# Row maxima of seven head pairs from the high parts alone, as 64-row products, four to a task

## Chip, core and metric

The kernel runs on one core of one Trainium2 chip. The metric is the device time of one launch in microseconds (us). The time before is 666.66 us, the median of 3 runs (666.63 to 666.75).

## The reference

Sixteen heads (two batches of eight) of pooled attention, then two dense two-layer networks over 1152 tokens of width 512:

```python
q_pool = q.reshape(B, H, S // 2, 2, D).mean(axis=3)          # 1152 queries become 576; D = 64
scores = scale * np.matmul(q_pool, k.transpose(0, 1, 3, 2))  # 576 x 1152 a head
scores = scores - np.max(scores, axis=-1, keepdims=True)
attn = np.exp(scores); attn = attn / (np.sum(attn, axis=-1, keepdims=True) + 1e-09)
out = np.matmul(attn, v)
# x = the heads side by side, 1152 x 512
# layer 1: max(0.01 h, h) with h = x @ w_in (512 x 2048), then @ w_out
# layer 2: h * sigmoid(h), same sizes
```

The maximum that is subtracted cancels in the quotient. It only has to be near enough to the row's maximum to keep the exponentials in range.

## The kernel before

The heads are worked in eight pairs p = 0 to 7; the two heads of a pair are j = 0 and j = 1. TensorE multiplies in the type fp32r, and each operand is split into a high part and a low part. For head j the tile `K2[p, j]` holds the high part of k on its own 64 rows (`own[j]`: rows 0 to 63 for j = 0, 64 to 127 for j = 1) and the low part on the other 64. `QH[p, j]` holds the high part of q twice, on both halves, so that one 128-row product gives high times high plus low times high. The own halves are written by ScalarE (ACT) from the loaded data ("at home"); the other halves come by DMA from there. `QL` and `KA` hold the low part of q, a row with minus the row maximum, and ones, for a second product.

Per pair, in the program's order of dependence:

- **Maxima** (`max_tile`, line 566). For pairs 1 to 7, 27 units, each one PSUM bank: 24 units are one product of 128 q rows by 384 keys (L586), twelve for each head; three "tail" units (L582, L583) take the last 64 q rows of both heads. VectorE (DVE) reduces each bank to one column of `mx` (L590). The q rows of a unit lie four apart (`t:NFC:NFULL`), so that the weights are read from SBUF with a stride of four elements. A unit depends on both halves of `QH` and `K2`, DMA'd parts included. `finish_max` (L634) joins three key chunks to `mn`, and a DMA writes it as a row into `QL`.
- **Scores** (`scores`, L675). Per key tile t and head two tasks of two products (128 x 288 each), then an exponential on ACT (L679) that frees the bank.
- **Sums** of the exponentials on GpSimd (POOL, L696), and at the pair's end four small products with ones (`sums`, L741).
- **Products with v** (`pv`, L712), nine tasks a pair of four fp32 products, on column halves of the array.
- `prep` loads, splits and moves q and k of a later pair; weights of the two networks are converted on ACT and DVE in the stretch of pairs 4 to 7 (L130 to L147), in part in PSUM.

The two networks follow (L1080, L1151, L1200) and are not touched.

The order of the instructions is made at build time by `Plan.run`: a list scheduler with one clock per engine, weights and due times. At each step it gives each free engine, of the tasks whose inputs and tokens are there, the one due first. PSUM banks are tokens: six "bank" tokens serve maxima, scores, sums and conversions, two further banks hold the result of `pv`. Each engine then runs its instructions in that order, waiting on semaphores.

Of the kernel before, what the change touches and what calls it, by code (L numbers as in the profile page):

```python
# [10 lines left out]
ALU = mybir.AluOpType  # L11
U32 = mybir.dt.uint32
W_TOP = 8053063168.0
AX = mybir.AxisListType
# [4 lines left out]
def pooled_attention_two_mlps(  # L19
# [27 lines left out]
    t=26.5,  # L47
# [3 lines left out]
    max=(-1.1, -0.35),  # L51
# [135 lines left out]
class Plan:  # L187
# [35 lines left out]

        self.rings[name] = (n, [], set())

    def can(self, x):
        if isinstance(x, str):
            return self.free[x] > 0
        n, taken, back = self.rings[x[0]]
        return len(taken) < n or taken[len(taken) - n] in back  # L230

    def run(self):
# [7 lines left out]
        while left:  # L240
            began = False
            for e in self.ENGINES:
                if idle[e] > now:
                    continue
                can = [t for t in ready[e] if t["at"] <= now and all(self.can(x) for x in t["take"])]
                if not can:
                    continue
                t = min(can, key=lambda t: (t["due"], t["n"]))
                for x in t["take"]:
                    if isinstance(x, str):  # L250
                        self.free[x] -= 1
                    else:
                        self.rings[x[0]][1].append(x)
                if t["emit"]:
                    t["emit"]()
                t["began"] = now
                ready[e].remove(t)
# [28 lines left out]
def attention(ctx, tc, q, k, v, xh, xl, weights, end_p):  # L286

    nc = tc.nc
# [35 lines left out]
    def bank():  # L324
        i = banks.pop(0)
        return psum[:, i], i
# [145 lines left out]
    def prep(p, loads, due, out):  # L472
# [58 lines left out]
        for j in range(2):  # L531
# [11 lines left out]
            for i in range(2):  # L543
                out["k", j, i] = a + bs
                out["kh", j, i] = a
            out["qu", j] = [cs, cs]
            out["qh", j] = cs
            out["ql", j] = [e]
        for name, ts in users.items():
# [13 lines left out]

    def max_tile(p, n, out, due):
        u, c = divmod(n, NCH)
        ks = slice(c * KC, (c + 1) * KC)
        deps = []
        for j in (0, 1) if u == NFULL else (0,) if u < NFULL else (1,):  # L570
            x = u if u <= NFULL else u - NFULL - 1

            deps += out["qu", j][0 if x < 2 else 1]
            deps += out["k", j, 0 if c == 0 else 1]

        def pe():
            if p not in mx:
                mx[p] = sm_p.tile([128, NM], F32, tag="mx", name="mx")
            box["max", p, n] = bank()
            ps = box["max", p, n][0]  # L580
            if u == NFULL:
                nc.tensor.matmul(out=ps[:, 0:KC], lhsT=QH[p, 1][:, SQ - 128:SQ], rhs=K2[p, 1][:, ks], start=True, stop=True)  # L582
                nc.tensor.matmul(out=ps[0:HALF, 0:KC], lhsT=QH[p, 0][:, NFC:SQ], rhs=K2[p, 0][:, ks], start=True, stop=True)  # L583
            else:
                j, t = (0, u) if u < NFULL else (1, u - NFULL - 1)
                nc.tensor.matmul(out=ps[:, 0:KC], lhsT=QH[p, j][:, t:NFC:NFULL], rhs=K2[p, j][:, ks], start=True, stop=True)  # L586

        def dve():
            ps, i = box.pop(("max", p, n))
            nc.vector.tensor_reduce(out=mx[p][:, n:n + 1], in_=ps[:, 0:KC], op=ALU.max, axis=AX.X)  # L590
            banks.append(i)

        t = add("PE", 0.35 if u == NFULL else 0.18, due, pe, after=deps, take=("bank",))
        return add("DVE", 0.56, due - 1.0, dve, after=[t], give=("bank",))

    def max_unit(u2, out, due, after):

# [247 lines left out]
    for p in range(NP):  # L845
# [12 lines left out]
        maxima = {}  # L858
        for u in range(2 * NFULL + 1 if p == 0 else 0):
            max_unit(u, out, 1.0 + 1.4 * u, filled[0])  # L860
        for n in range(NM if p else 0):
            lo, hi = P["max"]
            due = at(lo + (hi - lo) * n / NM)
            j, u = n // NA, n % NA // NCH
            maxima.setdefault((j, u), []).append(max_tile(p, n, out, due))
        for j in range(2 if p else 0):
            after = scored.get((p - 3, j), []) + (filled[p] if p < 3 else [])
            us = list(range(NFULL + 1 - j))
# [427 lines left out]
```

## Time and profile before

| | us |
|---|---|
| median of 3 runs | 666.66 |
| span of the profiled execution | 664.7 |
| attention, to the first product of the networks | 259.4 |
| one pair, from one set of sums to the next | 29.5 |
| PE busy | 646.1 (97%) |
| POOL busy | 392.0 (59%) |
| DVE busy | 441.3 (66%) |

The execution's own time outside its span is not shown; the median lies 2.0 us above the span. PE is TensorE, PEld its weight loads, which run under the products before. A row of the order of time gives the start, the time from the first start to the last end, the engine, the line, what is written and read, rows x columns of the weights, and how many instructions were joined. Since products overlap in the pipeline (a score product lasts 0.29 us, and the next begins 0.13 us after it), what a product costs TensorE is read from start to start, not from its length.

### The profile page before, as it was taken

How to read it: one execution, taken by the hardware profiler on the slowest of the kernel's cores; microseconds unless marked ns; L12 is line 12 of the kernel's file. 1: busy time of each engine (PE TensorE's matmuls, PEld its weight loads, DVE VectorE, ACT ScalarE, POOL GpSimd, SP SyncE). 2: the span in 40 equal slices, each digit the busy share in tenths (PEclk: the TensorE clock that was granted, in tenths of full speed). 3: DMA queues.
4: the chain of work that ended last, by engine and by line, in shares of the span. 5: the costliest groups of instructions: out<-in, count | busy, mean ns of one | idle time of the engine just before them, and what ended most of it. 6: DMA issues, size and time to landing. Idle time of an engine off the chain costs nothing.

```text
span 664.7 us, 9922 instructions
## 1 busy us (share of the span) xinstructions
PE 646.1 (97%) x3616; PEld 534.6 (80%) x3616; DVE 441.3 (66%) x614; ACT 326.8 (49%) x661; POOL 392.0 (59%) x278
## 2 busy tenths in 40 slices
PE   4889999999999998999999999999999999999997
PEld 3666777777777766988988988999988998888986
DVE  7284756678878766875676676698988888522222
ACT  4655766758686566554533433355456534312110
POOL 8657888897999833644544544476656453522120
PEclk9789999999999999999999999999999999999999
DMA  8636455455944130132233223232233322000012
GB/s 213 139 107 149 126 152 145 116 163 136 263 120 135 52 97 19 63 101 92 94 95 96 96 96 95 96 96 76 83 96 128 103 88 96 0 1 1 0 48 95
DMA packets 27959, 65.87 MB, mean 99 GB/s; under 512 B 9324, under 2 KB 9352, under 8 KB 27912
## 3 DMA queue, kind: packets, MB, share of 16 engines
q1 hardware_dynamic: 27912, 65.26, 33.7%
q8 instruction: 28, 0.46, 0.3%
q14 instruction: 19, 0.16, 0.1%
HBM read 49.81 MB, written 2.42 MB: 79 GB/s over the span
## 4 chain that ended last, share of the span: by engine, by line
PE 93%; POOL 2%; DMA 1%; ACT 1%; DVE 1%; issue 1%; SPq 0%; ACTq 0%; POOLq 0%; DVEq 0%
PE ph L1080 30%; PE po L1151 15%; PE pf L1200 15%; PE psum L675 12%; PE psum L712 11%; PE psum L586 7%; DMA k<-e 1%; PE psum L741 1%; DMA knat<-in_k_dram 1%; PE psum L583 1%; PE psum L582 1%; POOL k L439 0%; POOL e L504 0%; ACT qh L350 0%; ACT k L350 0%
## 5 line engine op out<-in xcount | busy, mean ns | idle before, releaser
L1133 POOL TENSOR_TENSOR gl<-a,gh 128x512 fp32r<-128x512 f32 (+1 forms) x64 | 97.3, 1520 | 143.1 <-ACT gh L1127 76.4
L696 POOL TENSOR_TENSOR acc<-acc,e 128x576 f32<-128x576 f32 x98 | 147.4, 1529 | 24.2 <-ACT e L679 23.8
L590 DVE TENSOR_REDUCE mx<-psum 128x1 f32<-128x384 f32 x189 | 96.5, 550 | 61.9 <-PE psum L586 55.7
L679 ACT ACTIVATE e<-psum 128x288 f32<-128x288 f32 x288 | 101.3, 414 | 69.8 <-PE psum L675 52.0
L1080 PE MATMUL ph<-xh,w0h 128*128 128x320 f32 (+1 forms) x384 | 109.0, 338 | 1.7 <-ACT pvs L727 1.7
L1080 PE MATMUL ph<-xl,w0h 128*128 128x320 f32 (+1 forms) x384 | 108.7, 337 | 0.0
L1080 PE MATMUL ph<-xh,w0l 128*128 128x320 f32 (+1 forms) x384 | 108.7, 337 | 0.0
L675 PE MATMUL psum<-qh,k 128*128 128x288 f32 x288 | 88.3, 323 | 1.7 <-ACT e L679 1.7
L712 PE MATMUL psum<-e,vnat 128*64 128x288 f32 x576 | 85.9, 423 | 0.0
L675 PE MATMUL psum<-ql,ka 128*128 128x288 f32 x288 | 81.8, 300 | 0.5 <-DMA ql<-mn 0.5
L675 PEld LDWEIGHTS psum<-qh,k 128*128 128x128 f32 x288 | 56.4, 196 | 26.3 <-issue 13.6
L1080 PEld LDWEIGHTS ph<-xh,w0h 128*128 128x128 f32 x384 | 67.7, 188 | 9.3 <-ACT pvs L727 2.2
L134 DVE TENSOR_SCALAR wt<-wt 128x512 f32<-128x512 f32 x56 | 40.3, 720 | 50.0 <-ACT wt L130 50.0
L1080 PEld LDWEIGHTS ph<-xh,w0l 128*128 128x128 f32 x384 | 66.9, 188 | 5.6
L1080 PEld LDWEIGHTS ph<-xl,w0h 128*128 128x128 f32 x384 | 66.9, 188 | 5.0
L169 POOL TENSOR_TENSOR w1l<-wt,w1h 128x512 fp32r<-128x512 f32 x32 | 44.4, 1398 | 39.1 <-ACT w1h L165 39.1
L586 PE MATMUL psum<-k,qh 128*128 128x384 f32 x168 | 62.8, 442 | 1.8 <-DMA k<-e 1.4
L169 POOL TENSOR_TENSOR w0l<-wt,w0h 128x512 fp32r<-128x512 f32 x32 | 44.7, 1396 | 24.3 <-ACT w0h L165 24.3
L138 DVE TENSOR_SCALAR wt<-wt 128x512 uint32<-128x512 uint32 x56 | 57.8, 1033 | 1.6
L712 PEld LDWEIGHTS psum<-e,vnat 128*64 128x64 f32 x576 | 35.8, 138 | 27.3 <-issue 12.0
L586 PEld LDWEIGHTS psum<-k,qh 128*128 128x128 f32 x168 | 47.1, 318 | 12.5 <-issue 4.9
L1106 ACT ACTIVATE gh<-ph 128x512 fp32r<-128x512 f32 (+1 forms) x32 | 20.9, 652 | 72.6 <-PE ph L1080 72.6
(89 smaller groups left out, 1162.8 us busy)
## 6 DMA issues: line engine op xcount, KB each, us to landing
wraw<-in_moe_w_in_dram SPq DMA_DIRECT2D x32, 512.0 KB, 3.9
wraw<-in_moe_w_out_dram SPq DMA_DIRECT2D x32, 512.0 KB, 3.3
vnat<-in_v_dram SPq DMA_DIRECT2D x8, 576.0 KB, 4.2
ka<-k SPq DMA_DIRECT2D x14, 288.0 KB, 5.2
knat<-in_k_dram SPq DMA_DIRECT2D x6, 576.0 KB, 6.0
qnat<-in_q_dram SPq DMA_DIRECT2D x6, 576.0 KB, 4.9
k<-knat SPq DMA_DIRECT2D x12, 288.0 KB, 3.3
out_dram<-acc SPq DMA_DIRECT2D x9, 256.0 KB, 2.0
```

The lines of the kernel that those rows point to most:

```text
L138: nc.vector.tensor_scalar(out=t, in0=t, scalar1=4, scalar2=1, op0=ALU.logical_shift_left, op1=ALU.logical_shift_right)
L169: self.nc.gpsimd.tensor_tensor(out=lo, in0=tf, in1=hi, op=ALU.subtract)
L586: nc.tensor.matmul(out=ps[:, 0:KC], lhsT=QH[p, j][:, t:NFC:NFULL], rhs=K2[p, j][:, ks], start=True, stop=True)
L590: nc.vector.tensor_reduce(out=mx[p][:, n:n + 1], in_=ps[:, 0:KC], op=ALU.max, axis=AX.X)
L675: nc.tensor.matmul(out=ps[:, 0:C], lhsT=lhsT[:, ks], rhs=rhs[:, cs], start=not last, stop=last)
L679: nc.scalar.activation(out=e_t[p, j, t][:, cs], in_=ps[:, 0:C], func=ACTF.Exp, scale=scale)
L696: e.tensor_tensor(out=acc[p, j], in0=e_t[p, j, 0] if t == 1 else acc[p, j], in1=e_t[p, j, t], op=ALU.add)
L712: nc.tensor.matmul(out=vps[p, c][own[j], 0:C], lhsT=vnat[p][:, j, t, :], rhs=e_t[p, j, t][:, c * C:(c + 1) * C], start=(t == 0), stop=(t = ...
L1080: nc.tensor.matmul(out=box[x][:, c, 0:n], lhsT=wt[:, kk, fs], rhs=m[:, kk, chunk(g, c)], start=(kk == 0 and wt is wh and m is xh), stop=(k ...
L1133: nc.gpsimd.tensor_tensor(out=gl, in0=box["a", x], in1=gh, op=ALU.subtract)
L1151: nc.tensor.matmul(out=box[x][:, c, 0:n], lhsT=wt[:, f, ms], rhs=y[:, c * n:(c + 1) * n], start=(f == 0 and wt is oh and y is gh), stop=(f ...
L1200: nc.tensor.matmul(out=box[x][:, 0, :], lhsT=y[:, ts], rhs=wt[:, f, :], start=(f == 0 and y is gh and wt is oh), stop=(f == FB - 1 and y i ...
```

## The change

For pairs 1 to 7 a product of the maxima (now L585) takes only the head's own 64 rows of `QH` and `K2`, which hold the high parts. Head 0 uses rows 0 to 63 of the array, head 1 rows 64 to 127. Four products, two query units of both heads for one key chunk, make one task that takes four bank tokens at once, and four tasks on DVE reduce them. So a pair has six such tasks and three tails (unchanged). The tasks depend only on the at-home halves and no longer on the DMAs. `Plan.can` is made to count tokens. The planner's weight for a task of four is 0.6, where a single product had 0.18. Numbers and sizes of products and reductions stay as they were: 168 products, 42 tails, 189 reductions.

```diff
-            out["qu", j] = [cs, cs]
+            out["qu", j] = cs
+            out["qh0", j] = [at_home["q", j]]
...
-    def max_tile(p, n, out, due):
-        u, c = divmod(n, NCH)
+    def max_tile(p, us, c, out, due):
...
+        tail = us == (NFULL,)
+        tiles = [(u, j) for u in us for j in ((1,) if tail else (0, 1))]
         deps = []
...
+        for j in range(2):
+            deps += (out["qu", j] if tail else out["qh0", j]) + out["k" if tail else "kh", j, 0 if c == 0 else 1]
...
-                nc.tensor.matmul(out=ps[:, 0:KC], lhsT=QH[p, j][:, t:NFC:NFULL], rhs=K2[p, j][:, ks], start=True, stop=True)
...
+            for u, j in tiles:
+                ps, _ = box["max", p, u, c, j] = bank()
...
+                    nc.tensor.matmul(
+                        out=ps[:, 0:KC], lhsT=QH[p, j][own[j], u:NFC:NFULL], rhs=K2[p, j][own[j], ks], start=True, stop=True,
+                    )
...
+        t = add("PE", 0.35 if tail else 0.6, due, pe, after=deps, take=("bank",) * len(tiles))
...
+        groups = [(us, c) for us in ((0, 1), (2, 3), (NFULL,)) for c in range(NCH)]
```

On TensorE, in the middle of a pair (scores of pair 3, maxima of pair 4), two places. Before (L586 maxima, L675 scores, L712 pv):

```order
L586 MATMUL psum<-k_858,qh_859 128x384 x2
L675 MATMUL psum<-qh_573,k_572 128x288
L675 MATMUL psum<-ql_104,ka_103 128x288
L675 MATMUL psum<-qh_573,k_572 128x288
L675 MATMUL psum<-ql_104,ka_103 128x288
L586 MATMUL psum<-k_858,qh_859 128x384 x2
L712 MATMUL psum<-e,vnat 64x288 x4
```

After (L585 maxima, L682 scores, L719 pv):

```order
L719 MATMUL psum<-e,vnat 64x288 x4
L585 MATMUL psum<-k_876,qh_877 128x384
L585 MATMUL psum<-k_878,qh_879 128x384
L585 MATMUL psum<-k_876,qh_877 128x384
L585 MATMUL psum<-k_878,qh_879 128x384
L682 MATMUL psum<-qh_596,k_595 128x288
L682 MATMUL psum<-ql_99,ka_98 128x288
L682 MATMUL psum<-qh_596,k_595 128x288
L682 MATMUL psum<-ql_99,ka_98 128x288
L719 MATMUL psum<-e,vnat 64x288 x4
```

Twos of one head between scores have become fours that alternate between the heads. Of the 42 tasks 30 stand right behind a pv, three behind the sums, eight behind scores or tails and one behind another task.

On TensorE where the scores of pair 5 end and those of pair 6 begin. Before, with two of pair 7's products on either side; the last product for pair 6's maxima stands 12 score tasks and three pv tasks ahead of pair 6's first score:

```order
L586 MATMUL psum<-k_1785,qh_1786 128x384 x2
L712 MATMUL psum<-e,vnat 64x288 x4
L675 MATMUL psum<-qh_1455,k_1454 128x288
L675 MATMUL psum<-ql_101,ka_97 128x288
L675 MATMUL psum<-qh_1455,k_1454 128x288
L675 MATMUL psum<-ql_101,ka_97 128x288
L586 MATMUL psum<-k_1785,qh_1786 128x384 x2
```

After (k_1457 and k_1459 are pair 6, k_1817 and k_1819 pair 7; L748 are the sums of pair 5):

```order
L719 MATMUL psum<-e,vnat 64x288 x4
L582 MATMUL psum<-k_1819,qh_1820 128x384
L583 MATMUL psum<-k_1817,qh_1818 64x384
L582 MATMUL psum<-k_1819,qh_1820 128x384
L583 MATMUL psum<-k_1817,qh_1818 64x384
L582 MATMUL psum<-k_1819,qh_1820 128x384
L583 MATMUL psum<-k_1817,qh_1818 64x384
L585 MATMUL psum<-k_1457,qh_1458 128x384
L585 MATMUL psum<-k_1459,qh_1460 128x384
L585 MATMUL psum<-k_1457,qh_1458 128x384
L585 MATMUL psum<-k_1459,qh_1460 128x384
L748 MATMUL psum<-acc,ones 32x288 x4
```

The last task of pair 6's maxima now stands behind all scores of pair 5 and behind pair 7's tails; after the sums come eight products for pair 7, and then pair 6's first score, which needs those maxima.

On DVE at the same boundary. Before, with pair 6's two joins (L634) apart:

```order
L590 TENSOR_REDUCE mx<-psum 128x1 x2
L634 TENSOR_REDUCE mn_1887<-mx 128x5
L590 TENSOR_REDUCE mx<-psum 128x1 x3
L776 RECIPROCAL cmp<-cmp 128x9
L590 TENSOR_REDUCE mx<-psum 128x1 x2
L504 TENSOR_TENSOR knat<-knat,kf 128x1152
L590 TENSOR_REDUCE mx<-psum 128x1 x4
L134 TENSOR_SCALAR psum<-psum 128x512
L634 TENSOR_REDUCE mn_1983<-mx 128x4
```

After (L594 reductions, L641 joins):

```order
L594 TENSOR_REDUCE mx<-psum 128x1 x4
L827 TENSOR_TENSOR xl<-pvs,xh 128x576
L147 SCALAR_TENSOR_TENSOR wt<-wraw,psum 128x512
L594 TENSOR_REDUCE mx<-psum 128x1 x3
L134 TENSOR_SCALAR psum<-psum 128x512
L594 TENSOR_REDUCE mx<-psum 128x1 x4
L641 TENSOR_REDUCE mn_2078<-mx 128x5
L641 TENSOR_REDUCE mn_2080<-mx 128x4
```

The reductions come in fours, and both joins stand behind the last of them.

## Rows read from the trace of the kernel before

**Rows 1.** The page: busy time and share of the span of each engine.

```profile
PE 646.1 (97%) x3616; PEld 534.6 (80%) x3616; DVE 441.3 (66%) x614; ACT 326.8 (49%) x661; POOL 392.0 (59%) x278
```

**Rows 2.** Busy time by stretch: length, five engines, granted clock, DMA share, GB/s.

```profile
63.88:93.38 29.50, 29.50 (x183) 21.42 (x182) 19.77 (x34) 19.73 (x47) 26.60 (x18) 1.00 0.47 133
181.90:211.40 29.50, 29.50 (x184) 21.60 (x183) 23.25 (x41) 21.57 (x51) 28.66 (x21) 1.00 0.49 136
```

**Rows 3.** TensorE in order of time inside one pair: start, length, line, joined.

```profile
100.94 0.67 PE L586 MATMUL psum<-k,qh 128*128 128x384 f32 x2
101.45 0.30 PE L675 MATMUL psum<-qh,k 128*128 128x288 f32 x1
...
101.84 0.29 PE L675 MATMUL psum<-ql,ka 128*128 128x288 f32 x1
102.07 1.19 PE L712 MATMUL psum<-e,vnat 128*64 128x288 f32 x8
103.19 0.80 PE L586 MATMUL psum<-k,qh 128*128 128x384 f32 x2
103.83 0.29 PE L675 MATMUL psum<-qh,k 128*128 128x288 f32 x1
...
105.23 1.19 PE L712 MATMUL psum<-e,vnat 128*64 128x288 f32 x8
106.35 0.40 PE L675 MATMUL psum<-qh,k 128*128 128x288 f32 x1
106.58 0.30 PE L675 MATMUL psum<-ql,ka 128*128 128x288 f32 x1
```

**Rows 4.** Groups by shape, weight loads: strided (L586) and contiguous (L582); mean in ns.

```profile
L586 PEld LDWEIGHTS psum<-k,qh 128*128 128x128 f32 x168 | 47.1, 318 | 12.5 <-issue 4.9 <-DVE mx L590 3.1 <-ACT e L679 2.0
L582 PEld LDWEIGHTS psum<-k,qh 128*128 128x128 f32 x21 | 3.9, 188 | 0.3
```

**Rows 5.** TensorE in order of time around two tails.

```profile
67.65 0.29 PE L675 MATMUL psum<-ql,ka 128*128 128x288 f32 x1
67.78 0.34 PE L582 MATMUL psum<-k,qh 128*128 128x384 f32 x1
67.96 0.34 PE L583 MATMUL psum<-k,qh 128*64 128x384 f32 x1
68.13 0.33 PE L582 MATMUL psum<-k,qh 128*128 128x384 f32 x1
```

**Rows 6.** The four sums of a pair in order of time, products.

```profile
63.88 0.69 PE L741 MATMUL psum<-acc,ones 128*32 128x288 f32 x8
64.50 0.57 PE L586 MATMUL psum<-k,qh 128*128 128x384 f32 x1
```

**Rows 7.** Their weight loads in order of time.

```profile
63.87 0.16 PEld L741 LDWEIGHTS psum<-acc,ones 128*32 128x32 f32 x8 [0.18 <-issue]
```

**Rows 8.** The page's costliest groups on POOL, DVE and ACT in attention.

```profile
L696 POOL TENSOR_TENSOR acc<-acc,e 128x576 f32<-128x576 f32 x98 | 147.4, 1529 | 24.2 <-ACT e L679 23.8
L590 DVE TENSOR_REDUCE mx<-psum 128x1 f32<-128x384 f32 x189 | 96.5, 550 | 61.9 <-PE psum L586 55.7
L679 ACT ACTIVATE e<-psum 128x288 f32<-128x288 f32 x288 | 101.3, 414 | 69.8 <-PE psum L675 52.0
```

**Rows 9.** TensorE in order of time at pair 1's maxima.

```profile
34.79 1.74 PE L586 MATMUL psum<-k,qh 128*128 128x384 f32 x6 [1.41 <-DMA k<-e]
```

**Rows 10.** Busy time by stretch just behind them; the clock is third from last.

```profile
36.00:40.00 4.00, 4.00 (x16) 2.48 (x16) 3.02 (x8) 1.79 (x3) 2.77 (x2) 0.57 0.26 96
```

**Rows 11.** The tile of joined maxima: its reductions, and its DMAs' issue to landing.

```profile
L634 DVE TENSOR_REDUCE mn<-mx x14: 152/156/167, 51.8 to 228.8; 128x5 fp32r<-128x15 f32 x7, 128x4 fp32r<-128x12 f32 x7
...
DMA to landing us min/median/max: 1.8/2.1/3.5
```

**Rows 12.** Groups by shape on DVE, 22 to 245 us: two of its other steps.

```profile
L820 DVE TENSOR_TENSOR xl<-pvs,xh 128x576 fp32r<-128x576 f32 x6 | 7.0, 1160 | 0.9 <-ACT xh L819 0.6
L147 DVE SCALAR_TENSOR_TENSOR wt<-wraw,psum 128x512 uint32<-128x512 uint32 x8 | 5.5, 683 | 0.2
```

More of the change, by code (lines that the diff above doesn't have):

```diff
@@ L224, in ring, with can @@
         self.rings[name] = (n, [], set())
-    def can(self, x):
+    def can(self, x, n=1):
         if isinstance(x, str):
-            return self.free[x] > 0
+            return self.free[x] >= n
         n, taken, back = self.rings[x[0]]
@@ L244, in run @@
                     continue
-                can = [t for t in ready[e] if t["at"] <= now and all(self.can(x) for x in t["take"])]
+                can = [t for t in ready[e] if t["at"] <= now and all(self.can(x, t["take"].count(x)) for x in t["take"])]
                 if not can:
@@ L561, in copy_ka @@
             out["ka", j, 0] = out["ka", j, 1] = [dma(due, go, after=out["kh", j, 0] + after, lag=P["lag"] + 1.0)]
-    def max_tile(p, n, out, due):
-        u, c = divmod(n, NCH)
+    def max_tile(p, us, c, out, due):
         ks = slice(c * KC, (c + 1) * KC)
+        tail = us == (NFULL,)
+        tiles = [(u, j) for u in us for j in ((1,) if tail else (0, 1))]
         deps = []
[L570 to L574, printed above, removed]
+        for j in range(2):
+            deps += (out["qu", j] if tail else out["qh0", j]) + out["k" if tail else "kh", j, 0 if c == 0 else 1]
         def pe():
@@ L578, in pe, with dve, go @@
                 mx[p] = sm_p.tile([128, NM], F32, tag="mx", name="mx")
[L579 to L585, printed above, removed]
-                nc.tensor.matmul(out=ps[:, 0:KC], lhsT=QH[p, j][:, t:NFC:NFULL], rhs=K2[p, j][:, ks], start=True, stop=True)
[L588 to L594, printed above, removed]
+            for u, j in tiles:
+                ps, _ = box["max", p, u, c, j] = bank()
+                if tail:
+                    nc.tensor.matmul(out=ps[:, 0:KC], lhsT=QH[p, 1][:, SQ - 128:SQ], rhs=K2[p, 1][:, ks], start=True, stop=True)
+                    nc.tensor.matmul(out=ps[0:HALF, 0:KC], lhsT=QH[p, 0][:, NFC:SQ], rhs=K2[p, 0][:, ks], start=True, stop=True)
+                else:
+                    nc.tensor.matmul(
+                        out=ps[:, 0:KC], lhsT=QH[p, j][own[j], u:NFC:NFULL], rhs=K2[p, j][own[j], ks], start=True, stop=True,
+                    )
+        def dve(u, j):
+            n = NCH * u + c + (NA if j and not tail else 0)
+            def go():
+                ps, i = box.pop(("max", p, u, c, j))
+                nc.vector.tensor_reduce(out=mx[p][:, n:n + 1], in_=ps[:, 0:KC], op=ALU.max, axis=AX.X)
+                banks.append(i)
+            return go
+        t = add("PE", 0.35 if tail else 0.6, due, pe, after=deps, take=("bank",) * len(tiles))
+        return [
+            (0 if tail else j, u, add("DVE", 0.56, due - 1.0, dve(u, j), after=[t], give=("bank",))) for u, j in tiles
+        ]
     def max_unit(u2, out, due, after):
@@ L860, in attention @@
             max_unit(u, out, 1.0 + 1.4 * u, filled[0])
-        for n in range(NM if p else 0):
+        groups = [(us, c) for us in ((0, 1), (2, 3), (NFULL,)) for c in range(NCH)]
+        for n, (us, c) in enumerate(groups if p else ()):
             lo, hi = P["max"]
-            due = at(lo + (hi - lo) * n / NM)
-            j, u = n // NA, n % NA // NCH
-            maxima.setdefault((j, u), []).append(max_tile(p, n, out, due))
+            for j, u, t in max_tile(p, us, c, out, at(lo + (hi - lo) * n / len(groups))):
+                maxima.setdefault((j, u), []).append(t)
         for j in range(2 if p else 0):
```

## Prediction

> **What bounds the kernel now.** I read the busy times first, then their shares by stretch, then TensorE's row in order of time. TensorE is busy 97% of the span [rows 1]. A middle pair takes 29.5 us, and TensorE is busy for all of it at the full clock, as it is in a late pair [rows 2]. So what a maxima product costs TensorE in a pair is what it costs the kernel, until another engine ends last. The nearest is POOL: 26.6 of 29.5 us in the middle pair, 28.7 in the late one, where it also splits weights [rows 2]. DVE and ACT stand at 19.8 and 19.7 us in the middle, 23.3 and 21.6 late.
>
> The reader is to look at starts. Two maxima products between scores begin at 100.94 and the next score at 101.45: 0.51 us for two, 0.255 each [rows 3]. A score product of 288 columns takes 0.13 us, so 384 columns alone would take 0.13 x 384/288 = 0.17 to 0.18, and the tails, also 384 columns, do take 0.17 to 0.18 [rows 5]. The difference is the weight load: with its stride of four it takes 318 ns, the contiguous one of the tails 188 [rows 4]. Maxima products go at the pace of their loads.
>
> **The change part by part.** The sum is made on the median: the profiled execution's own time is known only as its span of 664.7, 2.0 below the median, and all that changes lies inside the span.
>
> Removed: 168 products, in 84 twos. A two between scores is 0.51. Behind a pv it takes 0.64 (103.19 to 103.83), but of that the first product after a pv pays 0.10 in any case (0.23 from 106.35 to 106.58 where 0.13 is usual), so 0.54 net [rows 3]. About one two in four is of that kind: 84 x 0.5175 = 43.5 us.
>
> Added: 42 tasks of four products. Nothing in the trace has products on row halves. What one costs depends on two things.
>
> First, whether the halves run at once. The bounds are two product times or four for a task. The nearest rows are of column parts. Four products on four 32-column parts go from 63.88 to the next product at 64.50 in 0.62 us, and four of the same 288 columns on two 64-column parts from 102.07 to 103.19 in 1.12 us [rows 3, 6]. Twice as many parts take about half the time, so parts of the array do run together; the eight weight loads of the four also fit in 0.16 us [rows 7]. I take it that row halves do likewise, loads included, because a half's load then fills rows of its own as a column part's fills columns of its own. A task then costs what a two costs now: 0.51, or 0.54 behind a pv or the sums. By the order 33 tasks stand there and 9 elsewhere: 33 x 0.54 + 9 x 0.51 = 22.4 us. The gain is 43.5 - 22.4 = 21.1. If the loads of half the rows went faster than a full one, a pair of products would be bound by its 0.175 us of columns where I count 0.255; 42 x 2 x 0.08 = 7 more would be gained, and POOL's 28.7 us would not let the late pairs have all of it.
>
> Second, whether TensorE must empty itself where the shape of its parts changes. The nearest rows are the tails: there a full-width product is followed by one on 64 columns of the array and the next full one, at 67.78, 67.96 and 68.13, with steps of 0.18 and 0.17 [rows 5]. That is the pace of the columns, so the change of shape costs nothing there. Farther is the step into pv (0.23 from 101.84 to 102.07 where 0.13 is usual) and out of it (the 0.10 above) [rows 3]; those change the data type as well. I take nothing, by the nearer row; the other end is in the first rival.
>
> Moved, pair 1's start. Its maxima waited 1.41 us for the DMA k<-e, and the clock then stood at 0.57 from 36 to 40 us [rows 9, 10]. The new tasks need only the at-home copies and go among pair 0's scores; the tails that still need the DMA come after four of the tasks. That takes the wait away. Up to 1.7 of the slow stretch (4 us x 0.43) may go too, and some tasks now fall into the slow stretch before 30 us. I take -1.5 in all, between 0 and -3.
>
> Moved, the boundary of pairs 5 and 6. By the order the last task for pair 6's maxima stands behind all scores of pair 5. From the start of the task before it DVE has: 0.4 until the first product is out, four reductions (2.2), L827 (1.16), L147 (0.68), three reductions for tails (1.65), L134 (0.68 like L147), four reductions (2.2), two joins (0.3), and then the DMA lands 2.1 later [rows 8, 11, 12]. The sum is 11.4 us until pair 6's first score may start. TensorE has in that time: the task (0.54), a pv with its way in and out (1.3), three tails (3 x 0.35), the last task (0.54), the sums (0.85 with ways in and out), two tasks for pair 7 (1.1): 5.4 us. It waits 6.0. Bounds: 3 if the conversions have run early, 7.7 with a slow clock after the wait as in [rows 10].
>
> The boundary of pairs 6 and 7 has the same form with more behind it: four score tasks and two pv, 4.2 us with the task, against 0.4 + 2.2 + 0.3 + 2.1 = 5.0: 0.8. The other boundaries have three or four pv and eight to sixteen score tasks between the last maxima and the next pair's scores, over 8 us, and cost nothing.
>
> Moved, the banks. A task holds four of six banks until DVE has reduced them, 4 x 0.55 = 2.2 us [rows 8]. Scores behind it share two banks; a bank is bound for 0.27 of products, 0.41 of the exponential [rows 8] and 0.2 of handing over (an estimate, from a product that lasts 0.30 at a pace of 0.13 [rows 3]), so a score task comes every 0.44 instead of 0.27. If TensorE had only scores to do, it would lose 40% of that time. Scores fill a third of a pair (72 x 0.133 = 9.6 of 29.5), and 42 x 2.2 x 0.33 x 0.4 = 12 us is the upper end; zero is the lower, since most tasks stand behind a pv, which gives DVE and ACT 1.1 us, and about half are followed by at most two scores and then a pv or tail. I take 3.5, half a microsecond a pair.
>
> Nothing is added on DVE, ACT or the DMA queues: the same 189 reductions and the same moves. Accuracy of the maximum does not enter the time.
>
> Sum: 666.66 - 21.1 - 1.5 + 6.0 + 0.8 + 3.5 = 654.4; I say 654.5. Its own range is 645 (no bank waits, short boundary) to 662 (12 of bank waits).
>
> **The rivals.** *The array empties itself at each change of shape.* Then coming out of a task costs 0.10 of emptying, as the step into pv, and 0.10 for a first load that nothing hides, as the step out of it; this falls on all 42. The nine that don't stand behind a change of type pay 0.10 for going in, too, and 0.13 for their own strided load (0.64 against 0.51): 33 x 0.20 + 9 x 0.43 = 10.5 [rows 3]. The time is 665.0. For it: row parts are not column parts. Against it: the tails. The Trainium skill, page TensorEngine Tiling (Array Packing), section Tiling Modes, Key Properties, says that changing the tiling mode drains TensorE. By that the time would be this rival's; the tails' rows do not agree with it.
>
> *The halves do not overlap*, because loads or products of the two heads follow one another: this is the slower one. A task costs 1.05 behind a pv (0.64 + 0.51 - 0.10) and 1.02 elsewhere, 33 x 1.05 + 9 x 1.02 = 43.8, and nothing is gained: 654.5 + 21.4 = 675.9, less about 2 of bank waits that a slower TensorE hides, 674. It decides from 0.80 us a task on: the gain of 21.1 + 1.5 less the 10.3 of waits is 12.3, which is 0.29 a task over 0.53. For it: the strided load is what bounds now, and if it is bound by one reading path, halving the rows does not help. Against it: the sums.
>
> *Each task waits for a bank.* A task needs its four banks within half a microsecond, DVE gives one back every 0.55, and its other steps (1.16 and more) come in between. One reduction late per task is 42 x 0.55 = 23 instead of 3.5: 674. For it: DVE's share in late pairs. Against it: the order puts tasks behind a pv. The same page of the Trainium skill warns, under Gotcha 1, of more PSUM pressure with row tiling; no row here shows row tiles.
>
> **How the numbers follow.** My forecast has 0.52, the emptying array 0.22, no overlap 0.16, the banks 0.10. A measurement of this kernel can tell 0.2% (1.3 us) from no change. Nearly all of the first case is faster; of the second 0.12 is faster, 0.07 the same, 0.03 slower, since it lies 1.7 below with several us of doubt; the last two are slower but for 0.03. That gives faster 0.65, same 0.09, slower 0.26. Eight in ten: from 645, the low end of the forecast, to 673, which leaves out about half of the two slow cases and the deepest gains.
>
> **What would show it.** In the trace of the changed kernel the two products of heads 0 and 1 begin within some 20 ns of each other, and a task takes 0.5 to 0.55 from its first start to the next score; a middle pair takes 26.5 to 27.5 us. If a task takes 0.7 to 0.95 with the pairs of starts together, it is the first rival; if four starts lie 0.25 apart, the second; if TensorE's idle time is ended by the reductions again and again, the third. At the start of pair 6's scores there is a wait of 3 to 8 us ended by the DMA of the maxima, and none before pairs 2 to 5. The wait for k<-e is gone. I am wrong if the halves follow one another, or if waits at more boundaries than one eat the gain.

## The result, and the profile after

The changed kernel takes 669.86 us (median; 669.31 to 672.13) where the kernel before takes 666.7: ratio 1.0053, 95% interval 1.0035 to 1.007. The forecast was 654.5 us. The profiled execution has a span of 667.2 (before 664.7) and a mean clock of 0.988. Lines of the kernel after, in attention: L585 maxima, L594 their reductions on DVE, L682 scores, L686 exponentials, L719 pv, L748 sums, L703 POOL's sums of exponentials.

The page's busy line, to be set against [rows 1]:

```profile
PE 643.8 (97%) x3616; PEld 518.7 (78%) x3616; DVE 434.9 (65%) x614; ACT 324.3 (49%) x661; POOL 393.7 (59%) x278
```

TensorE is still busy 97%, and only 2 us less in all: the tasks save more, but slow stretches of the clock, shown below, make other products longer. Two tasks in TensorE's order of time (start, length, line), as [rows 3]:

```profile
93.05 1.19 PE L719 MATMUL psum<-e,vnat 128*64 128x288 f32 x7
94.16 0.80 PE L585 MATMUL psum<-k,qh 64*128 64x384 f32 x4
94.89 0.40 PE L682 MATMUL psum<-qh,k 128*128 128x288 f32 x1
95.12 0.29 PE L682 MATMUL psum<-ql,ka 128*128 128x288 f32 x1
95.26 0.29 PE L682 MATMUL psum<-qh,k 128*128 128x288 f32 x1
```

Four products take 0.73 us (94.16 to 94.89), and the first step behind them is 0.23 where 0.13 or 0.14 is usual. Inside a task the products start at 0, 0.00, 0.40 and 0.41 (medians): the two heads run at once, the second pair begins 0.40 behind the first. A task costs 0.73 behind a pv (the step of 0.23 is paid there in any case) and 0.93 between scores, where the way in takes 0.225 for 0.133 and the first score behind it pays 0.1 as well.

Then where the time goes. Until pair 5's scores begin, the changed kernel is ahead: the first scores of pairs 2 to 5 start at 84.7, 113.0, 142.6 and 172.4 us, before at 89.0, 118.5, 148.0 and 177.7, with the same 52, 76, 100 and 124 products of maxima done. Pair 6's first score is 3.9 late (211.1 for 207.2). One pair, from its first score to the next pair's, loses 9.3 us; before, then after:

```profile
177.74:207.22 29.48, 29.48 (x184) 21.48 (x183) 22.71 (x43) 21.77 (x50) 28.64 (x21) 1.00 0.59 159
```

```profile
172.40:211.14 38.74, 36.31 (x203) 23.01 (x201) 32.11 (x55) 23.07 (x54) 32.36 (x22) 0.92 0.61 164
```

Some of the 9.3 is work that stands earlier in the new order: pair 7's three tails, one more task and the sums of pair 5, about 2.4 us. The rest is waits and slow clock. TensorE in order of time at three waits, the first of them at pair 1's start, the others in that pair:

```profile
40.70 0.29 PE L682 MATMUL psum<-ql,ka 128*128 128x288 f32 x1
44.21 0.61 PE L682 MATMUL psum<-qh,k 128*128 128x288 f32 x1 [3.21 <-ACT e L686]
...
187.62 0.29 PE L682 MATMUL psum<-ql,ka 128*128 128x288 f32 x1
190.02 0.40 PE L682 MATMUL psum<-qh,k 128*128 128x288 f32 x1 [2.10 <-DVE mx L594]
...
204.20 0.56 PE L585 MATMUL psum<-k,qh 64*128 64x384 f32 x1
205.06 1.49 PE L585 MATMUL psum<-k,qh 64*128 64x384 f32 x3 [0.29 <-DVE wt L147]
206.55 1.09 PE L748 MATMUL psum<-acc,ones 128*32 128x288 f32 x8
207.56 3.65 PE L585 MATMUL psum<-k,qh 64*128 64x384 f32 x8
211.14 0.61 PE L682 MATMUL psum<-qh,k 128*128 128x288 f32 x1
```

ScalarE (ACT) ahead of the first:

```profile
38.33 0.69 ACT L350 ACTIVATE qnat<-qnat 128x576 fp32r<-128x576 f32 x1 [2.32 <-POOL qnat L480]
38.92 1.37 ACT L350 ACTIVATE qh<-qnat 64x576 fp32r<-64x576 f32 x2
40.32 1.17 ACT L350 ACTIVATE kf<-knat 128x1152 fp32r<-128x1152 f32 x1
41.39 2.33 ACT L350 ACTIVATE k<-knat 64x1152 fp32r<-64x1152 f32 x2
43.75 2.53 ACT L686 ACTIVATE e<-psum 128x288 f32<-128x288 f32 x8
```

VectorE (DVE) ahead of the second:

```profile
186.74 2.75 DVE L499 TENSOR_TENSOR qnat<-qnat 128x576 fp32r<-128x576 f32 x1
189.42 0.55 DVE L594 TENSOR_REDUCE mx<-psum 128x1 f32<-128x384 f32 x1
```

At 44.21 the score waits for a bank that an exponential frees, and the exponential stands on ACT behind pair 2's preparation, 5.4 us in a row from 38.33. Before, the same preparation began at 38.18, and TensorE had pair 1's maxima to do there [rows 9, 10]. At 190.02 the bank is freed by a reduction that stands on DVE behind a subtraction of 2.75 us. From 204.20 to 211.14 three tasks wait bank by bank for DVE, and the next pair's first score comes late. Busy time by stretch has the clock third from last, below 1.00 behind each of the three; in the other two rows nothing stops, and POOL, the fifth figure, is full:

```profile
40.00:50.00 10.00, 6.52 (x32) 3.64 (x30) 3.02 (x3) 6.92 (x14) 6.44 (x5) 0.83 0.50 118
...
70.00:80.00 10.00, 10.00 (x69) 6.91 (x65) 5.97 (x12) 7.60 (x17) 10.00 (x7) 1.00 0.66 177
...
170.00:180.00 10.00, 9.96 (x68) 5.99 (x65) 7.80 (x14) 6.91 (x18) 10.00 (x8) 1.00 1.00 224
...
190.00:200.00 10.00, 9.98 (x56) 6.32 (x56) 5.81 (x8) 5.17 (x15) 8.44 (x6) 0.83 0.65 171
...
210.00:220.00 10.00, 9.96 (x50) 7.26 (x50) 7.58 (x16) 4.72 (x12) 2.84 (x3) 0.76 0.23 55
```

### The profile page after: what moved, and what is told of

It is laid out like the page before. It is cut to its first block, busy times and chain, and to the rows that moved or that the text cites. A ratio compares the mean times of both kernels' runs of the same rounds, so it can differ in the third digit from the quotient of the medians.

```text
span 667.2 us, 9923 instructions
## 1 busy us (share of the span) xinstructions
PE 643.8 (97%) x3616; PEld 518.7 (78%) x3616; DVE 434.9 (65%) x614; ACT 324.3 (49%) x661; POOL 393.7 (59%) x278
## 4 chain that ended last, share of the span: by engine, by line
PE 90%; DVE 4%; ACT 2%; issue 1%; DMA 1%; SPq 0%; POOL 0%; ACTq 0%; DVEq 0%; POOLq 0%
PE ph L1087 30%; PE po L1158 15%; PE pf L1207 15%; PE psum L682 13%; PE psum L719 10%; PE psum L585 4%; DVE mx L594 2%; PE psum L617 1%; DVE mn L622 1%; DMA qnat<-in_q_dram 1%; PE psum L748 1%; ACT k L350 1%; ACT e L686 1%; PE psum L582 0%; DMA qh<-qh 0%
## 5 line engine op out<-in xcount | busy, mean ns | idle before, releaser
L703 POOL TENSOR_TENSOR acc<-acc,e 128x576 f32<-128x576 f32 x98 | 149.0, 1550 | 14.5 <-ACT e L686 13.9
L594 DVE TENSOR_REDUCE mx<-psum 128x1 f32<-128x384 f32 x189 | 93.1, 549 | 59.5 <-PE psum L585 49.3
L686 ACT ACTIVATE e<-psum 128x288 f32<-128x288 f32 x288 | 97.9, 420 | 64.7 <-PE psum L682 56.6
L682 PE MATMUL psum<-qh,k 128*128 128x288 f32 x288 | 91.8, 337 | 7.4 <-ACT e L686 4.7
L719 PE MATMUL psum<-e,vnat 128*64 128x288 f32 x576 | 86.8, 426 | 0.0
L682 PEld LDWEIGHTS psum<-qh,k 128*128 128x128 f32 x288 | 56.0, 195 | 34.8 <-issue 12.0
L682 PE MATMUL psum<-ql,ka 128*128 128x288 f32 x288 | 82.3, 303 | 0.0
L719 PEld LDWEIGHTS psum<-e,vnat 128*64 128x64 f32 x576 | 36.3, 138 | 28.1 <-issue 13.0
L682 PEld LDWEIGHTS psum<-ql,ka 128*128 128x128 f32 x288 | 56.6, 196 | 0.0
L1207 PE MATMUL pf<-w1h,gl 128*128 128x512 f32 x144 | 56.2, 390 | 0.0
```

The costliest lines, as they stand in the source:

```text
L682: nc.tensor.matmul(out=ps[:, 0:C], lhsT=lhsT[:, ks], rhs=rhs[:, cs], start=not last, stop=last)
L686: nc.scalar.activation(out=e_t[p, j, t][:, cs], in_=ps[:, 0:C], func=ACTF.Exp, scale=scale)
L703: e.tensor_tensor(out=acc[p, j], in0=e_t[p, j, 0] if t == 1 else acc[p, j], in1=e_t[p, j, t], op=ALU.add)
L719: nc.tensor.matmul(out=vps[p, c][own[j], 0:C], lhsT=vnat[p][:, j, t, :], rhs=e_t[p, j, t][:, c * C:(c + 1) * C], start=(t == 0), stop=(t = ...
L1207: nc.tensor.matmul(out=box[x][:, 0, :], lhsT=y[:, ts], rhs=wt[:, f, :], start=(f == 0 and y is gh and wt is oh), stop=(f == FB - 1 and y i ...
```

## Experiments

### Do the halves overlap, and what does a task cost?

All four products on rows 0 to 63:

```diff
-  lhsT=QH[p, j][own[j], u:NFC:NFULL], rhs=K2[p, j][own[j], ks]
+  lhsT=QH[p, 0][own[0], u:NFC:NFULL], rhs=K2[p, 0][own[0], ks]
```

> The changed kernel with all four products of a task on rows 0 to 63 (head 0's operands for both heads; so head 1 is shifted by head 0's maxima, which cancels in the quotient). The order of the instructions is that of the changed kernel. If products run together because they lie on different halves, the starts are 0.23 to 0.41 apart here, a task takes 1.05 to 1.3 instead of 0.73, and the kernel is 8 to 20 us slower than the changed one: 678 to 690. If two 64-row products run together wherever they lie, as the run with head by head could also mean, starts and time are those of the changed kernel, 670.

679.11 us, ratio 1.0191 [1.0173, 1.021], 9.2 slower than the changed kernel. TensorE's row:

```profile
92.33 1.26 PE L585 MATMUL psum<-k,qh 64*128 64x384 f32 x4
93.52 0.69 PE L748 MATMUL psum<-acc,ones 128*32 128x288 f32 x8
```

A task takes 1.19, its products start at 0, 0.40, 0.64 and 0.87. So the overlap comes from the two halves, as expected. Of 42 x 0.46 = 19 us of added work 9.2 reach the time.

The two products of a head one behind the other in the program:

```diff
-  tiles = [(u, j) for u in us for j in ((1,) if tail else (0, 1))]
+  tiles = [(u, j) for j in ((1,) if tail else (0, 1)) for u in us]
```

> The changed kernel with the four products of a task in the order head 0, head 0, head 1, head 1. If the halves overlap because neighbouring products lie on different halves, the first pair no longer starts together: a task takes 0.40 + 0.40 + 0.32 = 1.1 instead of 0.72, 42 x 0.4 = 16 us of TensorE's time, and the kernel is 6 to 16 us slower than the changed one. If the starts lie together for another reason, the time is the same, 669.9.

670.57, 1.0064 [1.0041, 1.0088]: no different from the changed kernel, and starts at 0, 0.01, 0.41, 0.41. The expectation's main case, 6 to 16 us slower, was a miss: the halves pair up whatever their order in the task. (The trace does not name the half of a product; that two on one half start 0.4 apart is the run before.)

### The order: tasks of four, and what they wait for

Tasks of four that wait for the moved rows, as the twos did before: in one kernel with products of all 128 rows (both edits), in another with row halves (the first edit alone):

```diff
-  deps += (out["qu", j] if tail else out["qh0", j]) + out["k" if tail else "kh", j, 0 if c == 0 else 1]
+  deps += out["qu", j] + out["k", j, 0 if c == 0 else 1]
...
-  lhsT=QH[p, j][own[j], u:NFC:NFULL], rhs=K2[p, j][own[j], ks]
+  lhsT=QH[p, j][:, u:NFC:NFULL], rhs=K2[p, j][:, ks]
```

> The changed kernel with its tasks of four and its planner, but each product of the maxima over all 128 rows as before, and the old dependence on the DMA'd halves (so the order of the instructions is that of e5_old_deps). If the order and the hold on four banks alone cost time (theory of the waits), this is slower than before by 8 to 14 us, since its products are those of before: 675 to 681. If they cost nothing, it is as before, 667. A task should take 0.25 to 0.28 a product (1.0 to 1.05 in all), its first start 0.13 behind a score, and the score behind it should pay nothing extra.

> The changed kernel with the old dependence alone: 64-row products, tasks of four, but they wait for the DMA'd halves again. Against e1_fours_full_rows only the rows differ. If halves overlap and emptying the array takes back half of it, a task takes 0.72 here against 1.0 to 1.05 there: 42 x 0.3 = 12.6 us of TensorE's time, of which the waits keep a part: 4 to 12 us faster than e1. Against the changed kernel: 0 to 4 us slower if the early start of pair 1 helps, and as much faster if it only moves the wait.

685.18, 1.0274 [1.0259, 1.029], and 680.61, 1.0214 [1.0175, 1.0252]. Grouping alone, with the products of before and the order that the planner makes of it, costs 18 us; 8 to 14 were expected. The first kernel is also the control for the change of shape. Its tasks go in and out at the usual pace (from the score behind a task to the next start it is 0.14 here, 0.24 behind row halves), and its last product takes 0.235 to the next start, where that of row halves takes 0.32:

```profile
117.97 1.27 PE L585 MATMUL psum<-k,qh 128*128 128x384 f32 x4
119.08 0.30 PE L682 MATMUL psum<-qh,k 128*128 128x288 f32 x1
119.22 0.29 PE L682 MATMUL psum<-ql,ka 128*128 128x288 f32 x1
```

Row halves save TensorE some 10 us against it (a task behind a pv takes 0.73 for 1.11, less the 0.1 of the score behind), and 4.6 reach the time. The changed kernel is 10.7 faster still, where 0 to 4 were expected; its only edit against the second is the dependence on the at-home copies, but that gives a new order throughout, so the 10.7 are not shown to be pair 1's start alone.

Tasks of two products, one of each head, that take two banks:

```diff
-  groups = [(us, c) for us in ((0, 1), (2, 3), (NFULL,)) for c in range(NCH)]
+  groups = [(us, c) for us in ((0,), (1,), (2,), (3,), (NFULL,)) for c in range(NCH)]
```

> The changed kernel with tasks of two products (one unit of both heads) instead of four: 84 tasks, two banks each. If emptying the array is the larger loss, twice as many changes of shape cost TensorE 84 x (0.32 to 0.52) = 27 to 43 us against 32 for the fours, and the time is 667 to 676. If the hold on four banks is the larger loss, the waits of some 14 us fall to 5 or less and the time is 660 to 667.

667.84, 1.0014 [1.0005, 1.0024]. Its TensorE work is about that of before or more (a two costs 0.50 and both ways, some 0.69 between scores); that fewer banks held at once make up for it is the likely reason, not shown by itself.

A planner that keeps banks free for a due task of four, so that no scores slip in ahead of it:

```diff
+  short = [x["due"] for x in ready["PE"] if x["at"] <= now and x["take"].count("bank") > 1]
+  if short and min(short) < t["due"] and t["take"].count("bank") == 1:
+      can = [x for x in can if "bank" not in x["take"] or x["take"].count("bank") > 1]
...
```

> The changed kernel with one more rule in the planner: while a task of four is ready on TensorE and due earlier, nothing due later takes a single bank. By the order at least 14 score tasks then stand between a pair's last maxima and its first scores at every boundary (0, 4 and 8 at the boundaries of pairs 6, 7 and 1 in the changed kernel). TensorE's own work stays as in the changed kernel, some 11.4 us under that of before by starts in the two traces. If starved tasks at the boundaries make the loss, the waits fall from some 14 us to 3 to 7, and the time is 658 to 662. If each task's hold on four banks makes it, wherever it stands, the time stays at 666 to 670.

672.38, 1.0088 [1.0066, 1.0111]. 658 to 662 was expected if late tasks at the pairs' boundaries make the loss. That theory fell: now 17 tasks stand between scores, they take 0.94 in the median, and nine of them wait for banks inside.

### Is POOL the next bound?

The kernel before with contiguous maxima products (a two takes 0.35 for 0.51 of [rows 3], some 13 us less for TensorE; no row halves). The edit has a second part, not shown here: the row of maxima is then written by six more DMAs a pair.

```diff
-  lhsT=QH[p, j][:, t:NFC:NFULL]
+  lhsT=QH[p, j][:, t * 128:(t + 1) * 128]
```

> The kernel before with one change: the q rows of a maxima unit are 128 neighbours, so the weight load reads without a stride; the row of maxima is then written by one DMA per unit (nine more than before reduced to four: six more DMAs a pair). If the strided load sets the pace of the 128-row products, a two between scores takes 0.35 to 0.38 instead of 0.51, 168 x 0.07 to 0.08 = 12 to 13 us go from TensorE, and the time is 653 to 658. If the load is hidden, 667. If the further DMAs come late, there are waits before each pair's scores and up to 2 us a pair come back.

665.69, 0.9991 [0.9976, 1.0005]. 653 to 658 was expected; nearly nothing of 13 us comes out, without any change of shape or grouping. That made POOL the suspect: in this kernel it is at 10.00 of 10 in eight of the 24 stretches of 10 us from 20 to 260 (in the kernel before it is in two, in the changed one in six). So 14 sums of exponentials went from POOL to DVE, in the kernel before, the changed one and the contiguous one, and 28 in the changed one:

```diff
-    dve_add=(),
+    dve_add=((1, 0), (1, 1)),
```

> The kernel before with one edit: in pairs 0 to 6 the first sum of exponentials of each head (14 in all) is made by DVE (0.75 us each) instead of POOL (1.42 each). POOL has 20 us less to do, DVE 10.5 us more, TensorE's work is unchanged. Theory that POOL becomes the bound only where TensorE is relieved: TensorE is busy 97% of this kernel, so 664 to 668, within 0.4% of 666.9. Rival (the banks: DVE gives them back later and that is what stalls the scores): 668 to 674, since DVE has more to do. If this kernel alone is faster by over 4 us, POOL bounded the kernel before already.

> The changed kernel (669.9) with the same edit: 14 sums moved from POOL to DVE. Theory that POOL is the bound once TensorE is relieved: POOL is no longer at 10.00 of 10 in window after window, the stalls of the scores behind held tiles go, and of the 11.4 us that TensorE was relieved of most comes out: 656 to 662. Rival (four banks held by a task until DVE has reduced them): DVE has 10.5 us more, banks come back later, 670 to 676.

> The kernel before with contiguous maxima products (they take 0.35 a two where they took 0.51; that alone gave 665.7) and the same edit: 14 sums moved from POOL to DVE. No tasks of four, no row halves. Theory that POOL is the bound once TensorE is relieved: 653 to 659. Rival (the order, or DVE, is the bound): 664 to 670.

> The changed kernel with twice the dose: the first two sums of each head of pairs 0 to 6 (28 in all) made by DVE; POOL has some 41 us less to do than in the changed kernel, DVE 21 more. Theory that POOL is the bound once TensorE is relieved: with two moved sums a pair POOL is already well below the span, so the other two give little: within 3 us of the kernel with 14 moved sums, 655 to 662. Rival (banks and DVE): slower again than that one by 3 to 8 us, 673 to 682.

669.07 (1.0036 [1.0021, 1.005]), 664.91 (0.9974 [0.9963, 0.9985]), 665.74 (0.9985 [0.9967, 1.0002]) and 671.53 (1.0078 [1.0058, 1.0099]). The changed kernel gains 5 us, and 8 to 14 were expected if POOL is the bound; twice the dose loses 1.7 instead; the contiguous one gains nothing, where 7 to 13 were expected. POOL is not all of it, and how much of the 5 us is POOL and how much the new order is open.

### Pair 1's start

Pair 2's loads are planned to land later, so that its preparation stands behind pair 0's last exponentials on ACT; in the changed kernel without and with the 14 moved sums, in the one with tasks of two and in the contiguous one:

```diff
+  lag = 11.0 if p == 2 else 5.0
-  made["q"] = [dma(due + 0.1, q_part(None), take=("qnat",), lag=5.0, begin=begin)]
+  made["q"] = [dma(due + 0.1, q_part(None), take=("qnat",), lag=lag, begin=begin)]
```

> The changed kernel with one edit: the planner is told that pair 2's q and k land 11 us after their issue, where it takes 5, so that pair 2's preparation on ScalarE (5.4 us in a row from 38.3) is planned behind the exponentials of pair 0's last scores and not ahead of them. Theory that the change took away cover (pair 1's maxima used to keep TensorE at work there): the wait of 3.4 at 44.2 us goes and so does about 1 us of slow clock behind it: 664.5 to 667 where the changed kernel has 669.9. Rival (another engine bounds the pairs, so that time won at one place is given back at the next): 668.5 to 671.

> Both edits in the changed kernel: pair 2's preparation planned later, and 14 sums of exponentials moved from POOL to DVE (that alone gave 664.9, with a wait of 4.3 us at 42.4). If the two causes are separate they add: 659 to 662. Rival (the moved sums had already taken what there was, another engine bounds the rest): 663.5 to 666.

> The kernel with row halves but tasks of two products and two banks (667.8, with one wait of 3.1 us at 38.9 ended by an exponential), with pair 2's preparation planned later. Theory of the lost cover: 663 to 665.5. Rival (given back later): 667 to 669.

> The kernel before with contiguous maxima products (665.7; no row halves, pair 1's maxima still behind the moved rows) and pair 2's preparation planned later. There TensorE had pair 1's maxima as cover, its waits near that place were 1.5 (a DMA) and 1.2 (an exponential). Theory of the lost cover: at most the 1.2 goes, 664 to 666.5. Rival (the plan's wrong landing time costs every kernel): 661 to 663.5.

668.55 (1.0031 [1.0019, 1.0044]), 677.45 (1.0155 [1.0131, 1.0179]), 668.97 (1.0039 [1.0014, 1.0063]) and 664.70 (0.9966 [0.9951, 0.9981]). The wait did not go, it moved. TensorE's row of the first:

```profile
45.10 0.29 PE L683 MATMUL psum<-ql,ka 128*128 128x288 f32 x1
49.68 0.61 PE L683 MATMUL psum<-qh,k 128*128 128x288 f32 x1 [4.29 <-ACT e L687]
```

In both places of ACT's 5.4 us TensorE has only scores to do, since pair 1's maxima lie earlier. And with both edits, two gains became a loss of 12.5 against the moved sums alone, where 659 to 666 was expected: each new plan shifts waits of several us.

### What would tasks at no cost give?

Products left out, all else in its order: in the kernel before every second one (the edit shown), or all of them (with p < 0 for the condition), and in the changed kernel all of pairs 2 to 7 (with p < 2).

```diff
-            else:
+            elif n % 2 == 0:
                 j, t = (0, u) if u < NFULL else (1, u - NFULL - 1)
                 nc.tensor.matmul(out=ps[:, 0:KC], lhsT=QH[p, j][:, t:NFC:NFULL], rhs=K2[p, j][:, ks], start=True, stop=True)
```

> The kernel before with every second maxima product of pairs 1 to 7 left out (84 of 168; the reductions still run, on what the bank holds, so the maxima are not the reference's; the last 96 columns of each bank are set to zero once at the start). TensorE has 84 x 0.255 = 21.4 us less to do, just the gain that the forecast put on the change; the order of every engine is the same. If TensorE is the bound: 645 to 648. If the other engines and the written order take over: 656 to 665, with TensorE waiting.

> The kernel before with all 168 maxima products of pairs 1 to 7 left out (the reductions still run on what the banks hold). TensorE has 43.5 us less to do. If TensorE is the bound: 623 to 628. If other engines and the order hold the time from some point on: 648 to 662, little below the kernel with half of the products left out.

> The changed kernel with the maxima products of pairs 2 to 7 left out (36 of 42 tasks of four; the reductions still run on what the banks hold). TensorE has 36 x 0.73 to 0.93, some 27 to 30 us, less to do and no change of shape but the tails'; the order is the changed kernel's. If TensorE is the bound: 640 to 645. If the other engines and the order hold the time: 654 to 667, in other words the changed kernel could not have been much faster even with tasks that cost nothing.

656.13 (0.9839 [0.9825, 0.9854]), 652.45 (0.9781 [0.9765, 0.9798]) and 667.20 (1.0029 [0.9997, 1.006]). One stretch, 60 to 220 us, of before, the half, all, the changed kernel, and that with its products left out (TensorE, its loads, DVE, ACT, POOL, clock):

```profile
60.00:220.00 160.00, 160.00 (x988) 116.44 (x987) 118.00 (x204) 110.05 (x257) 138.61 (x94) 1.00 0.55 148
```

```profile
60.00:220.00 160.00, 157.99 (x982) 107.53 (x982) 124.20 (x221) 113.82 (x270) 150.96 (x101) 1.00 0.57 152
```

```profile
60.00:220.00 160.00, 149.84 (x939) 93.50 (x939) 125.11 (x222) 115.09 (x279) 154.19 (x105) 0.98 0.57 151
```

```profile
60.00:220.00 160.00, 155.81 (x963) 102.16 (x962) 112.79 (x205) 106.33 (x251) 137.64 (x92) 0.97 0.57 151
```

```profile
60.00:220.00 160.00, 135.44 (x842) 85.62 (x842) 119.42 (x207) 106.22 (x254) 136.16 (x92) 0.95 0.58 157
```

In the order of before, 21.4 us less work (by the forecast's price of 0.255; a product left alone between scores takes 0.28, so nearer 20) gives 10.7, the next 22 give 3.7, and POOL goes from 87% to 94% and 96%. With all left out POOL is what bounds the pairs. TensorE's longest sum of waits in these 160 us is at the pairs' sums, for POOL (what waits, what ends it, us in total, times, longest):

```profile
PE psum L741 <- POOL acc L696: 6.3, 7, 1.6
```

With half left out it is not: TensorE is busy for 158 of the 160 us, and none of its waits there is ended by POOL. Some 4 us of what is missing are lost at pair 1's start, where there are fewer maxima to cover ACT's preparation (before, then the half; the clock is third from last):

```profile
40.00:50.00 10.00, 9.62 (x44) 7.18 (x44) 9.96 (x19) 6.68 (x12) 5.13 (x3) 1.00 0.28 58
```

```profile
40.00:50.00 10.00, 7.84 (x28) 5.25 (x28) 7.34 (x15) 5.86 (x10) 3.53 (x3) 0.68 0.32 70
```

Pair 1's first score starts at 60.2 us for 59.5 before, though 14 products fewer stand ahead of it. What keeps the other 5 or so is not shown.

In the changed order, 27 to 30 us less work gives 2.7, and no engine is above 85%. There the order itself holds the time, with waits for DVE, ACT and POOL in turn, and the clock with it: it stands at 0.95 over the stretch, where the changed kernel has 0.97 and the kernel before 1.00, so up to 8 of the 160 us go with slow stretches. The waits in the whole of this run:

```profile
PE psum L682 <- DVE mx L594: 9.6, 6, 6.2
PE psum L682 <- ACT e L686: 9.4, 10, 2.7
...
PE psum L748 <- POOL acc L703: 5.1, 6, 2.5
```

## Why the forecast was wrong

**The halves run at once**: right. Starts are 3 ns apart, and with one half alone the task takes 1.19 for 0.73. By the forecast's own signs (pairs of starts together, a task of 0.7 to 0.95) it is the first rival that came.

**The array does not empty**: wrong. I priced the change of shape at nothing by the tails, which use fewer columns [rows 5]; products on row halves pay 0.09 from the last pair to the next start, 0.1 at the score behind, and between scores 0.09 on the way in and 0.40 for 0.255 at the first pair; full rows in the same tasks pay none of the ways in and out. (The 0.40 is not of the halves: a full-width product behind the sums takes it too, 64.50 to 64.90 before [rows 6].) 33 x 0.73 + 9 x 0.93 = 32.5 us for 22.4: the gain for TensorE is 11.0 and not 21.1. That is the first rival, 10.5 priced, 10.1 measured, and its parts fit too (0.19 a task for 0.20, 0.42 for 0.43 for the nine). The Trainium skill, page TensorEngine Tiling (Array Packing), section Tiling Modes, Key Properties, says that a change of the tiling mode drains TensorE. The tasks agree with it by 0.1 each way, the tails still do not.

**"What a maxima product costs TensorE in a pair is what it costs the kernel, until another engine ends last"**: this would have failed even with tasks as cheap as forecast, for I priced every us of TensorE's work as a us of time. Half of the products left out, about the gain of 21 that I forecast, gives 10.7, and all of them 14.4: a gain of 21 was not there to be had by cheaper products alone. I named POOL for the engine that ends last and gave it no price; it is that engine only with all left out. [Rows 2] did not have the cap: POOL leaves 2.9 us in that middle pair and 0.8 in that late one, but over 60 to 220 us it leaves 160 - 138.6 = 21.4, more than came out. With half left out, some 4 us were lost at pair 1's start, and the rest is open. In the changed kernel the middle pairs, forecast at 26.5 to 27.5, take 28.3, 29.6 and 29.8 from first score to first score, where 29.5 stood before.

**Pair 1's start**, -1.5: right in sign, about a third of the size, and by other waits than forecast. The wait of 1.41 went [rows 9], but the maxima that went with it were what TensorE did during ACT's preparation: there 3.2 us of waits came, and 0.3 ahead of them. What paid for it was not in the forecast: in the kernel before the first scores wait 0.55 for a DMA and 1.65 for an exponential (at 21.5 and 23.6 us), and pair 1's first task now runs in that place. TensorE's waits from 20 to 60 us, but for one of 0.4 that both have, are 4.0 before and 3.5 after; slow stretches are alike in both (at about 24 to 29 us before and 21 to 27 after, by the pace of the scores, and again behind 36.5 and 44.2), so about -0.5.

**The boundary of pairs 5 and 6**, +6.0: about right (204.2 to 211.1 for work of some 3 us, and the stretch at 0.76 behind it). **Banks held**, +3.5: the rows of TensorE show some 2.7 us at 102, 127 to 132 and 150. **A wait behind DVE's preparation**, at 190: 2.1 us and about 1.2 of slow clock, not forecast.

With these sizes the forecast's own sum is 654.4 + 10.1 + 1.0 (pair 1's start) + 3.3 (at 190) = 668.8, and 669.9 was measured. The nearness is in part luck, for the terms do not simply add: with the tasks at no cost the changed kernel keeps 667.2. Its order is 14.8 slower than that of before when both have their products left out (652.45; the changed kernel still has pair 1's six tasks, 4.4 to 5.6 us, and a clock of 0.95 for 0.98 over 60 to 220 us). So the emptying is what the rival said, and yet in the changed order even tasks at no cost would give little, for waits that the order makes stand behind it. Up to pair 5 the changed kernel was 5.3 us ahead; the waits at 190 and from 204 to 211 lost that and more. What share each cause has (four banks held until DVE has reduced them, a pair's last task behind the scores before, preparation ahead of reductions) stays open: each attempt to take one away moved the waits.

Two versions beat both kernels: the changed one with 14 sums on DVE (664.91), and, without row halves, the contiguous products with pair 2's preparation later (664.70).

## What to carry to other kernels

Before pricing relief of the busiest engine, leave the work out and measure: here leaving out half gave half of its price, and the other half 3.7 us. The room of the second busiest engine, summed over the stretches, is an upper bound only (21.4 us here, 14.4 came out). Before moving work earlier, look what long step of another engine it covers where it stands. Compare two orders where equal work is done: a loss that looks spread may sit in one pair. And price a change of the array's parts by rows of the same kind of part: the tails, a change of columns at no cost, did not tell the cost of a change of rows.

## What the runs showed of the hardware

A VectorE sum or difference of 128 x 576 with both inputs in SBUF takes 0.75 us while POOL is idle (all 18 at the end of attention in the changed kernel). While POOL works it takes 0.75 to 1.9 in the kernel before, the changed one and that with its products left out, and in two cases far longer: 2.75 and 6.87. In the changed kernel with its products left out, DVE in order of time:

```profile
181.84 6.87 DVE L499 TENSOR_TENSOR qnat<-qnat 128x576 fp32r<-128x576 f32 x1
188.64 0.55 DVE L594 TENSOR_REDUCE mx<-psum 128x1 f32<-128x384 f32 x1
```

POOL there:

```profile
177.23 5.58 POOL L703 TENSOR_TENSOR acc<-acc,e 128x576 f32<-128x576 f32 x4
182.76 1.28 POOL L169 TENSOR_TENSOR w0l<-wt,w0h 128x512 fp32r<-128x512 f32 x1
183.98 4.12 POOL L703 TENSOR_TENSOR acc<-acc,e 128x576 f32<-128x576 f32 x3
```

And TensorE:

```profile
189.24 0.61 PE L682 MATMUL psum<-qh,k 128*128 128x288 f32 x1 [6.22 <-DVE mx L594]
```

The subtraction ends 0.6 us after POOL's unbroken row of operations does, and TensorE has waited 6.2 us for the reduction behind it. The 2.75 us at 186.74 in the changed kernel have the same look: POOL works without pause to 188.87 there, and the subtraction ends at 189.49. The Trainium skill, page SBUF — State Buffer, section Who interferes with whom, says that a VectorE instruction with two SBUF inputs contends with a GpSimd instruction that reads SBUF. The rows agree (0.75 alone, 0.75 to 1.9 beside POOL but for the two), and in the longest case the VectorE instruction stood through the rest of one of POOL's instructions and four more. That the port is the cause there is argued, not shown: at 188.69 in the kernel before the same subtraction took 0.75 while POOL worked without pause. So a full POOL may cost twice: by its own time, and by what it makes of DVE's steps.

The halves pair up whatever the order of their products in a task. And a weight load with a stride of four sets the pace of a product (0.255 us), where a contiguous one leaves the columns to set it (0.176 in the contiguous kernel).
